# A fused attention and channel-mix kernel: a new hand-held order with more idle matmuls at the start, and last stores spread over two queues

## The chip, the core and the metric

The kernel runs on one core of a Trainium2 chip. The metric is the device time of one execution in microseconds; the time of a kernel is the median of its runs. The profile is one execution taken by the hardware profiler, and its times are counted from the start of that execution's span.

## What is computed

A linear attention with a normalised output feeds a channel mix with a squared ReLU and a sigmoid gate. The reference, cut to what matters:

```python
batch, n_heads, seq, head_dim = 8, 8, 576, 64      # d_model 512, d_ff 1024
kv  = einsum('bhsd,bhse->bhde', k, v)
att = einsum('bhsd,bhde->bhse', q, kv)
att = att / sqrt(mean(att * att, -1) + 1e-6) * g_norm
x   = att.transpose(0, 2, 1, 3).reshape(B, S, H * D)
x_prev = x shifted by one row of the sequence, zero at its start
xk = mu_k * x + (1 - mu_k) * x_prev
xr = mu_r * x + (1 - mu_r) * x_prev
kk  = maximum(xk @ w_k, 0)
out = sigmoid(xr @ w_r) * ((kk * kk) @ w_v)
```

All inputs and the output are float32 in memory; the loads issued by GpSimd (POOL) cast to bf16 on the way, and the matmuls run in bf16.

## The kernel before, in words

**Work and stages.** Attention runs batch by batch (b = 0 to 7), heads in four pairs (hp = 0 to 3). The channel mix runs over nine groups g of 512 rows, each group as soon as the batches that it needs are done. All bf16 tiles are held transposed, features on partitions.

- Loads: `load_q0.4` loads q of batch 0 from head 4 on (L281, POOL's queue). Batch 0 is loaded two heads at a time, batch 1 four heads at a time, later batches whole. Heads 0 and 1 of k and v of batch 0 come as float32 through SP's and ACT's queues (`early_k`, `early_v`, L291) and are cast on the chip (`cast_k`, `cast_v`, L294, by copy on L185 for ACT or L187 for VectorE, here DVE). `load_w_r`, `load_w_k`, `load_w_v` load each weight in two halves (L265).
- Attention of a head pair: `kv` is k transposed times v on TensorE (PE; L369 for batches 0 and 1, L354 later), `kvm` or `kvc` evicts it (L373, L361); `qT` transposes q on PE (L407, L412) and `qTc` evicts it (L416), from batch 3 on a DMA transpose on SP's queue does this (`qTd`, L395); `u` is q times kv (L431, L437), `uc` evicts it, in batch 0 scaled by g_norm (L456), `sq` squares it (L197, L199).
- Normalisation: in batch 0 `ss` sums the squares of a head pair with a matmul of ones (L482), `rs` is ACT's reciprocal root (L487), `x` multiplies (L491). Later batches do all four head pairs in one `st` (L520) and `rs` (L525), spread by the matmuls `sp` (L559) and multiplied by `x` (L564).
- Shift and blend: `d` is x minus the shifted x (L584, L585), `tk` and `tr` multiply it by mu (L191 on ACT, L193 on DVE), `xk` and `xr` add x (L595).
- Channel mix: `K` is xk times w_k (L630; K0.3 is group 0, feature block 3; blocks 0 to 3 need the first half of w_k, the others the second), `relu` (L634, ACT) and `sqk` (L637, DVE) follow; `R` is xr times w_r (L652), `sig` its sigmoid (L657, ACT); `V` is the square times w_v (L686, `a` with the first half of w_v, `b` with the second), `o` the product with the gate (L690, DVE), `S` the store (L616). In group 0 the R matmuls go head pair by head pair, so R0.0 needs only xr of head pair 0.

**What sets the order.** `ORDER`, a string of names, is the order in which the pieces are recorded, and each engine and queue runs its own in that order. After a name stand the engine (`A` ACT, `D` DVE, `S` SP) and the buffer slots: `qTc0.2:A:0` is on ACT and takes slot 0 of its tile. PSUM has four slots (`ps`), kv, q, k and v have two each, the float32 output tiles four. `Plan.run` (L96) only asks that what a piece needs stands before it and that the earlier users of a slot do. The costs in `add` (such as `{"ACT": 0.535, "DVE": 0.37}`) are a planner's; in this file only the order of the engines in such a dictionary has an effect, as the default where the name gives none.

**Idle matmuls.** `idle:28:0` issues 28 matmuls of a zero tile, 224 columns wide, into slot 0 of `ps`:

```python
def idle(n, slot):
    for _ in range(n):
        nc.tensor.matmul(tiles[("ps", slot)][:, 0, HS:512], zeros[:, 0:128], zeros[:, HS:512], start=True, stop=True)
```

Their result is never read. They wait for the zero tile (`zero`, L232) and for readers of the slot that they overwrite. Before the change there are 61 of them, in seven places, all ahead of R0.0.

**Stores.** A piece `S` stores 128 rows; in the last two groups it is cut in two (`.a`, `.b`), and each part can go to SP's or ACT's queue. In the last group each block of 128 rows has its own product, and the last block has two halves by columns (`o8.1.3.0`, `o8.1.3.1`).

Of the kernel before, what the change touches and what calls it, by code (L numbers as in the profile page):

```python
# [12 lines left out]


ORDER = """
    zero load_q1.4::0 ident load_v0.4::0 load_k0.4::0 early_k::0 g_load mu_r_load:A load_q0.4::1 idle:28:0 qT0.2::0 kv0.2::1
    ones kvm0.2::0 qT1.3::2 load_v0.6 load_k0.2 load_k0.6 load_q0.0 load_q0.6 load_v0.2 load_q0.2 load_v1.4::1 load_k1.4::1
    early_v::1 cast_v:A mu_k_load:S cast_k:A qTc0.2:A:0 kv0.0::3 u0.2::1 ident9 kvm0.0 mu_mm::0 mu sq0.2::0 qTc1.3:A:1 idle:9:3
    qT0.0::3 uc0.2:A:0 qTc0.0:D sel_load ss0.2::0 qT0.3::2 rs0.2::0 u0.0::1 qTc0.3:A idle:7:3 qT0.1::3 kv0.1::0 x0.2::0 d0.2::0
    tk0.2:D:0 qTc0.1:D sq0.0 ss0.0::2 rs0.0::1 kv0.3::3 kvm0.1 u0.1::0 qT1.2::2 sq0.1 uc0.0:D uc0.1:A load_q1.0 load_v1.0  # L20
    load_k1.0 idle:7:1 kv1.2::1 kvm0.3 x0.0 d0.0 tr0.0:D:1 u0.3::3 kvm1.2::1 tr0.2:D xk0.2 sq0.3 idle:3:0 u1.3::0 uc1.3:A:1
    ss0.1::1 rs0.1::0 uc0.3:D sel xr0.2 x0.1 d0.1 xr0.0 load_w_r0 qT1.0::0 ss0.3::3 qT1.1::1 qTc1.2:A qTc1.0:A rs0.3::1 qTc1.1:A
    tr0.1:D x0.3 idle:5:2 kv1.0::2 kvm1.0 d0.3 u1.2::0 tr0.3:A uc1.2:A xr0.1 load_w_r1 load_w_k0 idle:2:1 R0.0::31 u1.0::2 R0.1
    tk0.0:A tk0.3:D xk0.3 uc1.0:D xr0.3 xk0.0 tk0.1:D xk0.1 load_w_k1 R0.2 R0.3.1 R0.3.0 u1.1::0 sig0.0::0 sig0.1::1 uc1.1:D
    sq1.0:D:0 sq1.1:D K0.0::2 K0.1 K0.3::0 K0.2 st1::3 relu0.0::0 load_q2.0::1 load_w_v0 K0.5::1 sqk0.0::0 rs1::0 sp1.1::23
    x1.1.0::1 x1.1.1 load_w_v1 K0.4 K0.7::2 relu0.1::1 sqk0.1 relu0.2::0 sp1.0::03 K0.6 x1.0.0 x1.0.1 sqk0.2 qT2.2::1 relu0.3::1
    sqk0.3 V0.1a::0 V0.2a::3 qT2.1::2 V0.2b d1.0::0 qTc2.1:A:0 V0.3a qT2.3::2 tr1.0:A:1 d1.2 tr1.2:D xr1.2 xr1.0 V0.3b tk1.0:D:0
    o0.1::2 qTc2.3:A qT2.0::2 qTc2.0:A V0.0a load_k2.0::0 load_v2.0::0 R1.0::2 R1.1 kv2.0::3 tk1.2:A sig1.0::2 kvc2.0.0:A:0
    load_k3.0::1 load_v3.0::1 xk1.2 qTc2.2:D xk1.0 V0.0b kvc2.0.1:A K1.3::1 K1.2 V0.1b load_q3.0::0 qTd3::1 K1.6::2 o0.0::3
    relu1.1::0 kvc2.0.2:A u2.0::1 uc2.0:D:0 u2.1::3 uc2.1:A sq2.0:D:0 K1.7 u2.3::0 u2.2::3 relu1.3::1 uc2.2:A K1.4::1 K1.0::2  # L30
    K1.1 uc2.3:D sq2.1:D sqk1.3::1 sqk1.1 st2::0 rs2::1 relu1.0::1 sqk1.0 K1.5 relu1.2::0 R1.3::3 sp2.1::02 R1.2 load_q4.0::1
    V1.3a::1 V1.2a x2.1.1::0 x2.1.0 sqk1.2 sp2.0::20 sig1.1::1 x2.0.1 d2.2::0 tk2.2:A:1 load_v5.0::0 x2.0.0 V1.1a::3 V1.0a V1.0b
    kv3.0::0 load_v4.0::1 V1.3b V1.1b V1.2b d2.0 tk2.0:D xk2.0 xk2.2 K2.0::2 o1.0::1 kvc3.0.2:D:1 tr2.0:D:0 K2.1 K2.4::3 K2.5
    tr2.2:D xr2.2 relu2.0::1 xr2.0 kvc3.0.1:D sqk2.0::0 kvc3.0.0:D relu2.2::0 load_k4.0::0 K2.2::2 K2.3 R2.0::3 o1.1::0
    relu2.1::1 u3.0::0 u3.1::1 u3.2::2 R2.1 uc3.1:A:1 uc3.0:D sq3.0:A:0 sig2.0::0 R2.3::0 R2.2 sig2.1::2 u3.3::1 S1.2 qTd4::0
    uc3.2:D sqk2.2 sqk2.1 K2.6::2 kv4.0::3 load_v6.0::1 uc3.3:D sq3.1:D st3::1 S1.3 rs3::0 K2.7 kvc4.0.1:D:0 kvc4.0.2:D
    kvc4.0.0:D sp3.1::01 relu2.3::0 x3.1.1::1 x3.1.0 load_k5.0::1 V2.0a::3 V2.1a sp3.0::12 sqk2.3 u4.0::0 uc4.0:A:0 V2.1b x3.0.1
    S0.3 S0.2 x3.0.0 d3.2::0 d3.0 tk3.2:D:1 tr3.2:D:0 u4.3::2 u4.1::0 u4.2::1 uc4.1:A sq4.0:A:0 uc4.3:A uc4.2:A sq4.1:A V2.0b
    tr3.0:D xr3.2 load_q5.0::0 xr3.0 xk3.2 tk3.0:A V2.3a::0 V2.3b V2.2a V2.2b xk3.0 st4::2 rs4::1 R3.0::1 R3.1 K3.2::2 K3.3
    o2.1::0 o2.0::2 sig3.0::1 sp4.0::01 x4.0.1::0 x4.0.0 relu3.1::1 R3.2::3 R3.3 sp4.1::12 x4.1.1 K3.1::0 K3.0 x4.1.0 K3.5::2  # L40
    K3.7::1 K3.4 K3.6 d4.2::0 tk4.2:A:0 relu3.0::0 sig3.1::2 d4.0 tk4.0:D xk4.2 sqk3.1::1 xk4.0 kv5.0::0 relu3.2::1 sqk3.0
    relu3.3::0 kvc5.0.0:D:1 K4.2::3 K4.4::2 K4.5 K4.3 K4.7::1 K4.6 kvc5.0.1:A tr4.2:D:1 tr4.0:A sqk3.2 xr4.0 sqk3.3 qTd5::1 S2.2
    S2.3 S1.0 load_k7.0::0 load_k6.0::1 relu4.1::1 relu4.3::0 kvc5.0.2:D xr4.2 sqk4.1::0 relu4.2::1 sqk4.2 K4.1::3 K4.0
    relu4.0::1 V3.3a::0 V3.2a load_v7.0::0 load_q6.0::1 load_q7.0::0 u5.3::1 u5.1::2 V3.2b uc5.3:D:1 uc5.1:A u5.0::3 u5.2::1
    uc5.2:D sqk4.0 uc5.0:A sq5.0:D:0 V3.3b R4.3::2 o3.1::0 sqk4.3 S1.1 S0.1 S3.2 R4.2 sq5.1:A st5::3 rs5::0 V3.0a::1 sp5.0::03
    sig4.1::0 V3.0b V3.1a x5.0.1::1 x5.0.0 sp5.1::30 kv6.0::2 V3.1b x5.1.0 x5.1.1 d5.2::0 tk5.2:A:0 d5.0 tk5.0:D xk5.2 V4.3a::3
    R4.1::0 R4.0 V4.3b V4.2a kvc6.0.0:A:0 sig4.0::2 xk5.0 K5.2::0 V4.2b tr5.0:A:1 kvc6.0.1:A K5.3 tr5.2:A relu5.1::1 S0.0
    qTd6::0 o3.0::1 o4.1::3 S3.3 kvc6.0.2:D K5.0::1 xr5.2 K5.1 K5.6::3 relu5.0::0 sqk5.0::1 u6.1::2 u6.0::0 uc6.1:A:0 uc6.0:A
    K5.7 V4.1a::1 V4.1b u6.2::2 u6.3::0 relu5.3::0 uc6.2:A xr5.0 sq6.0:D:0 sqk5.1 uc6.3:D sq6.1:D V4.0a V4.0b o4.0::0 st6::3
    kv7.0::2 rs6::1 sp6.1::03 x6.1.0::0 x6.1.1 sqk5.3 kvc7.0.2:D:1 kvc7.0.1:D R5.1::1 R5.0 K5.5::0 K5.4 sig5.0::1 kvc7.0.0:D  # L50
    relu5.2::1 sp6.0::31 R5.2::2 R5.3 sig5.1::0 sqk5.2 x6.0.0 x6.0.1 d6.0::0 tk6.0:D:0 xk6.0 tr6.0:A:1 d6.2 tk6.2:D V5.1a::0
    xk6.2 V5.2a::3 V5.2b V5.1b qTd7::1 u7.2::2 u7.3::1 uc7.3:A:1 S4.1 S4.2 S3.1 S2.0 S2.1 S4.0 S4.3 uc7.2:A sq7.1:A:0 V5.0a
    V5.0b u7.1::1 u7.0::2 uc7.1:A uc7.0:A sq7.0:D V5.3a tr6.2:D o5.0::2 xr6.2 xr6.0 K6.3::1 K6.1::2 V5.3b o5.1::0 K6.2
    relu6.1::0 K6.0 relu6.0::1 sqk6.1::0 sqk6.0 K6.5::0 K6.4 st7::1 rs7::0 K6.6::3 K6.7 R6.2::2 relu6.2::0 S3.0 relu6.3::1
    sqk6.2 sp7.0::10 R6.3 x7.0.0::1 sqk6.3 x7.0.1 sig6.1::2 V6.2a::3 R6.0::1 sp7.1::02 x7.1.1 d7.2::0 x7.1.0 V6.3a V6.3b
    V6.1a::2 V6.2b V6.0a R6.1 V6.0b V6.1b d7.0 tk7.2:D:0 tk7.0:D xk7.2 tr7.0:D:1 xk7.0 sig6.0::1 o6.1::3 K7.3::0 K7.2 tr7.2:A
    relu7.1::0 sqk7.1::1 K7.4::1 K7.5 relu7.2::1 sqk7.2 o6.0::1 S6.2 S6.3 K8.0::3 K8.3::0 K8.2 S5.1 S5.0 S6.0 S6.1 K7.0::1
    relu8.1::0 sqk8.1::0 xr7.0 xr7.2 K8.1 K7.1 relu8.0::1 relu7.0::0 K8.4::2 sqk7.0 K7.7::0 K7.6 R8.2::3 R8.3 sig8.1::0
    relu7.3::0 sqk7.3 sqk8.0 R7.2::1 R7.3 sig7.1::2 R7.1::3 R7.0 K8.5 relu8.2::0 V7.2a::0 S5.3 V7.3a V7.3b K8.6::1 R8.0::2 K8.7
    V7.2b sig7.0::1 S5.2 relu8.3::1 o7.1::3 S7.3.b:S S7.2.a:A sqk8.2 V8.0a::3 V7.1a::1 sqk8.3 R8.1 V7.1b sig8.0::2 V7.0a  # L60
    V8.1a::0 V8.1b o8.0.1.0::2 V7.0b S8.1.1.0.a:S o7.0::1 V8.0b o8.0.0.0 V8.2a::2 V8.2b V8.3.0a::0 V8.3.0b V8.3.1a::1 V8.3.1b
    S7.0.a:A S8.0.0.0.b:A S7.0.b:A S7.1.b:A S8.1.1.0.b:S S7.2.b:S S7.1.a:S S8.0.0.0.a:S S7.3.a:S o8.1.2.0::0 S8.2.2.0.a:A
    S8.2.2.0.b:A o8.1.3.0 S8.3.3.0.a:A S8.3.3.0.b:S o8.1.3.1 S8.3.3.1.a:S S8.3.3.1.b:A
"""


# [51 lines left out]
def kernel(  # L118
# [499 lines left out]
    def mix(g):  # L618
# [73 lines left out]
        for c2 in range(2):  # L692
# [18 lines left out]
            for xs, cs, ms, tag, ps in todo:  # L711
                w = (xs[1] - xs[0]) * (cs.stop - cs.start)
                dv = add(f"o{g}.{c2}{tag}", {"DVE": 0.07 + 1.06 * w / 1024},
                         lambda _, xs=slice(*xs), ps=ps, sg=sg, ot=ot, cs=cs: v_mul(_, xs, ps, sg, ot, cs), deps=ms + [sg_done], bufs=[ps, sg, ot])
                for x in range(*xs):
                    ci = 2 * c2 + x
                    rows = runs(g, ci)
                    for i, part in enumerate([rows] if g < NG - 2 else [[r] for r in rows]):
                        on = {"SP": 0.53 * len(part)}
                        if g >= NG - 2:  # L720
                            on["ACT"] = 0.45
                        add(f"S{g}.{ci}{tag}" + (f".{'ab'[i]}" if g >= NG - 2 else ""), on,
                            lambda eng, ci=ci, ot=ot, x=x, cs=cs, part=part: store(eng, g, ci, get(ot)[:, x, :], cs, part), deps=[dv],
                            bufs=[ot], land=0.64 * sum(n for _, n in part) / 128 * (cs.stop - cs.start) / C)
# [44 lines left out]
```

## Time and profile before

| | us |
|---|---|
| median of 7 runs (210.82 to 212.48) | 211.81 |
| the profiled execution | 212.13 |
| its span | 210.3 |
| PE busy | 196.6 |
| DVE busy | 140.4 |
| ACT busy | 124.1 |
| first matmul of the channel mix's R (L652) | 27.21 |
| first matmul of its K (L630) | 31.38 |
| end of the last matmul | 204.19 |

The page cuts the span into 40 slices of 5.26 us; a digit is the busy share of an engine in a slice in tenths. PEclk is the TensorE clock that was granted, in tenths of the full one. Groups of rows are named by line, engine and tiles; `ps L630` is what line 630 writes. The timeline has start, duration, engine, line and tiles of instructions, neighbours of one kind merged; a `q` after the engine is its queue, which issues transfers, and the bracket is the idle time before and what ended it. A windows row has the stretch, its length, then busy time and count of each engine, the clock, the DMA share and the GB/s. A transfer's landing is given as us after its issue.

### The profile page before, as it was taken

The numbers are of one execution on the slowest core, as the hardware profiler recorded it, in microseconds if no ns is written. First come the engines' busy times: TensorE is split into PE (matmuls) and PEld (weight loads), VectorE is DVE, ScalarE is ACT, GpSimd is POOL, SyncE is SP. The second block draws the span as 40 slices with busy tenths as digits, with TensorE's granted clock in tenths as the row PEclk, the third lists the DMA queues.
The fourth block names the chain that finished last, engine by engine and source line by source line (L and its number), as shares of the span: only waits on it lengthen the run. The fifth ranks groups of instructions, "written<-read, shape, count | busy, mean of one in ns | idle before, by whom it ended". The sixth has DMA issues, their size and how long they took to land.

```text
span 210.3 us, 3834 instructions
## 1 busy us (share of the span) xinstructions
PE 196.6 (93%) x1538; PEld 98.2 (47%) x1559; DVE 140.4 (67%) x259; ACT 124.1 (59%) x149; POOL 29.4 (14%) x46
## 2 busy tenths in 40 slices
PE   7299999999999999999999999999999999999980
PEld 6276654445335444434783444354443444444440
DVE  2017995994959988988957794878685957122360
ACT  2245879487792386892977778765678065361100
POOL 7893530011002005000410000000000000000000
PEclk9857999999999999999999999999999999999996
DMA  6999999999980979998799998048100035400274
GB/s 147 190 197 203 205 205 206 206 201 203 191 100 5 174 154 181 195 205 102 146 195 260 219 229 122 0 126 225 51 0 0 3 111 169 123 3 0 62 209 127
DMA packets 39317, 29.71 MB, mean 141 GB/s; under 512 B 13564, under 2 KB 34820, under 8 KB 39300
## 3 DMA queue, kind: packets, MB, share of 16 engines
q0 software_dynamic: 21248, 16.48, 51.7%
q1 hardware_dynamic: 17020, 11.45, 24.3%
q10 hardware_dynamic: 1032, 1.54, 2.6%
q8 instruction: 12, 0.20, 0.4%
q14 instruction: 5, 0.04, 0.1%
HBM read 33.56 MB, written 9.44 MB: 204 GB/s over the span
## 4 chain that ended last, share of the span: by engine, by line
PE 89%; DMA 3%; ACT 2%; issue 2%; POOL 1%; DVE 1%; POOLq 0%
PE ps L630 30%; PE ps L686 29%; PE ps L652 14%; DMA q<-in_q_dram 3%; PE ps L354 3%; PE ps L437 2%; PE ps L736 2%; PE ps L407 2%; PE ps L369 2%; PE ps L559 2%; PE ps L431 1%; PE ps L520 1%; ACT sq L197 1%; PE ps L482 1%; ACT L205 1%
## 5 line engine op out<-in xcount | busy, mean ns | idle before, releaser
L686 PE MATMUL ps<-w_v,sqk 128*128 128x512 bf16 (+1 forms) x285 | 65.8, 373 | 0.9 <-issue 0.6
L630 PE MATMUL ps<-xk,w_k 128*128 128x512 bf16 (+1 forms) x313 | 65.7, 358 | 0.7 <-issue 0.5
L634 ACT ACTIVATE relu<-ps 128x1024 bf16<-128x1024 f32 x36 | 36.4, 1022 | 25.5 <-PE ps L630 17.2
L630 PEld LDWEIGHTS <-w_k 128*128 128x128 bf16 x320 | 30.3, 98 | 30.4 <-issue 1.6
L686 PEld LDWEIGHTS <-sqk 128*128 128x128 bf16 x296 | 27.5, 98 | 31.0 <-issue 1.4
L637 DVE TENSOR_TENSOR sqk<-relu 128x1024 bf16<-128x1024 bf16 x36 | 24.3, 687 | 16.5 <-ACT relu L634 16.5
L652 PE MATMUL ps<-w_r,xr 128*128 128x512 bf16 x141 | 34.2, 380 | 0.3 <-issue 0.2
L690 DVE TENSOR_TENSOR out<-ps,sig 128x1024 f32<-128x1024 f32 (+2 forms) x21 | 22.3, 1068 | 17.0 <-issue 10.8
L657 ACT ACTIVATE sig<-ps 128x1024 bf16<-128x1024 f32 x18 | 18.3, 1021 | 13.9 <-PE ps L652 13.7
L564 DVE TENSOR_TENSOR xT<-uT,ps 128x576 bf16<-128x576 bf16 x28 | 20.1, 750 | 6.6 <-PE ps L559 5.9
L191 ACT ACTIVATE t<-d,mu_sb 128x576 bf16<-128x576 bf16 x24 | 17.4, 767 | 10.3 <-DVE d L585 10.3
L652 PEld LDWEIGHTS <-xr 128*128 128x128 bf16 x144 | 13.3, 98 | 16.4 <-DVE xr L595 0.7
L185 ACT CAST uT<-ps 128x576 bf16<-128x576 f32 x18 | 11.0, 635 | 5.1 <-PE ps L437 5.0
L193 DVE TENSOR_SCALAR t<-d,mu_sb 128x576 bf16<-128x576 bf16 x40 | 13.2, 373 | 0.3
L595 DVE TENSOR_TENSOR xr<-t,xT 128x1152 bf16<-128x1152 bf16 (+1 forms) x18 | 11.9, 685 | 1.4 <-ACT t L191 1.4
L585 DVE TENSOR_TENSOR d<-xT 128x1152 bf16<-128x1152 bf16 (+1 forms) x18 | 12.4, 691 | 0.6
L281 POOL DMA_DIRECT2D v<-in_v_dram x11 | 7.9, 715 | 33.4 <-PE ps L354 32.3
L595 DVE TENSOR_TENSOR xk<-t,xT 128x1152 bf16<-128x1152 bf16 (+1 forms) x18 | 12.2, 687 | 0.3
L736 PE MATMUL ps<-zeros 128*128 128x224 bf16 x61 | 10.4, 339 | 1.2 <-DVE zeros L232 1.2
L281 POOL DMA_DIRECT2D q<-in_q_dram x12 | 8.6, 720 | 19.6 <-PE ps L412 13.5
L281 POOL DMA_DIRECT2D k<-in_k_dram x11 | 7.9, 716 | 22.0 <-PE ps L354 18.8
L187 DVE CAST uT<-ps 128x576 bf16<-128x576 f32 x10 | 7.5, 756 | 3.4 <-PE ps L437 3.1
(60 smaller groups left out, 137.3 us busy)
## 6 DMA issues: line engine op xcount, KB each, us to landing
out_dram<-out SPq DMA_DIRECT2D x20, 192.0 KB
q<-in_q_dram POOLq DMA_DIRECT2D x6, 576.0 KB, 14.9
k<-in_k_dram POOLq DMA_DIRECT2D x6, 576.0 KB, 14.8
v<-in_v_dram POOLq DMA_DIRECT2D x6, 576.0 KB, 11.3
out_dram<-out SPq DMA_DIRECT2D x20, 128.0 KB
out_dram<-out SPq DMA_DIRECT2D x23, 64.0 KB
w_k<-in_moe_w_k_dram POOLq DMA_DIRECT2D x2, 512.0 KB, 13.6
w_v<-in_moe_w_v_dram POOLq DMA_DIRECT2D x2, 512.0 KB, 16.3
```

Source lines behind the costliest of these rows:

```text
L191: nc.scalar.mul(out=dst, in_=src, mul=by)
L281: nc.gpsimd.dma_start(out=get(kvq[(n, b)])[:, h0:h1, :], in_=rows(n, b, h0, h1))
L564: nc.vector.tensor_tensor(out=get(xT)[:, 2 * i:2 * i + 2, NP + c:NP + c + HS], in0=flat(slice(2 * i, 2 * i + 2))[:, :, c:c + HS], in1=get( ...
L595: nc.vector.tensor_tensor(out=dst[:, hsl, c0:c0 + S], in0=get(t[key])[:, hsl, :], in1=get(xT)[:, hsl, 0:S], op=ALU.add)
L630: nc.tensor.matmul(get(ps)[:, fc % 2, a0:a1], w_k_sb[:, cc, 128 * fc:128 * fc + 128], xk[:, cc, x0:x0 + a1 - a0], start=(cc == 0), stop=(c ...
L634: nc.scalar.activation(out=get(rt), in_=get(ps), func=AF.Relu)
L637: nc.vector.tensor_mul(out=get(sqk)[:, 2 * f2:2 * f2 + 2, :], in0=get(rt), in1=get(rt))
L652: nc.tensor.matmul(get(ps)[:, ci % 2, :], xr[:, cc, c:c + 128], w_r_sb[:, cc, :], start=(cc == 0), stop=(cc == NHP - 1))
L657: nc.scalar.activation(out=get(sg), in_=get(ps), func=AF.Sigmoid)
L686: nc.tensor.matmul(get(ps)[:, ci % 2, cs], get(sqk)[:, fc, 128 * ci:128 * ci + 128], w_v_sb[:, fc, cs], start=(fc == 0), stop=(fc == NFC - 1))
L690: nc.vector.tensor_mul(out=get(ot)[:, xs, cs], in0=get(ps)[:, xs, cs], in1=get(sg)[:, xs, cs])
L736: nc.tensor.matmul(tiles[("ps", slot)][:, 0, HS:512], zeros[:, 0:128], zeros[:, HS:512], start=True, stop=True)
```

## The change

Only `ORDER` and two of the planner's costs change. The pieces are the same ones, each once, apart from the idle matmuls: 79 in ten places instead of 61 in seven, again all but one ahead of R0.0 (the one stands before R0.2).

- The first real work on PE is kv0.0, from the early loads, and then head pair 0; it was q's transpose and kv of head pair 2. `idle:28:0` stays first, and `idle:12:1` follows kv0.0.
- POOL's queue starts with k, q and q of heads 2, 2 and 0 of batch 0, and batch 1's first q comes seventh; it was first. `load_w_r0` stands before the k and v loads of batch 1; it stood behind them.
- The small loads swap queues: `mu_r_load` goes to SP, ahead of `early_k`, and `mu_k_load` to ACT, behind `early_v`, which is now ACT's first transfer. `cast_k` and `cast_v` go from ACT to DVE.
- ss, rs, x, d, t and the blends of batch 0 run in the order of head pairs 0, 1, 2, 3; they ran 2, 0, 1, 3. kv1.2, kv1.0, qT1.0, u1.2 and u1.3 now stand behind R0.0.
- Later stages keep their pieces in a new order of loads, stores, slots and engines. At the end the halves of a store go to SP and ACT in turn, and group 7's first product comes earlier than group 8's first.

The core of the diff (the start and the end of `ORDER`, and the costs):

```diff
-    zero load_q1.4::0 ident load_v0.4::0 load_k0.4::0 early_k::0 g_load mu_r_load:A load_q0.4::1 idle:28:0 qT0.2::0 kv0.2::1
-    ones kvm0.2::0 qT1.3::2 load_v0.6 load_k0.2 load_k0.6 load_q0.0 load_q0.6 load_v0.2 load_q0.2 load_v1.4::1 load_k1.4::1
-    early_v::1 cast_v:A mu_k_load:S cast_k:A qTc0.2:A:0 kv0.0::3 u0.2::1 ident9 kvm0.0 mu_mm::0 mu sq0.2::0 qTc1.3:A:1 idle:9:3
-    qT0.0::3 uc0.2:A:0 qTc0.0:D sel_load ss0.2::0 qT0.3::2 rs0.2::0 u0.0::1 qTc0.3:A idle:7:3 qT0.1::3 kv0.1::0 x0.2::0 d0.2::0
...
+    zero load_k0.2::0 early_v::0 mu_r_load:S early_k::1 mu_k_load:A g_load load_q0.2::0 load_q0.0 load_v0.2::0 load_v0.6
+    load_q0.4::1 load_q1.4::1 ident ones cast_k:D cast_v:D idle:28:0 kv0.0::0 sel_load kvm0.0::0 load_v0.4 load_k0.4 load_k0.6
+    load_q0.6 idle:12:1 qT0.0::1 qTc0.0:D:0 idle:7:0 u0.0::2 ident9 mu_mm::3 mu qT0.1::0 uc0.0:D:0 qTc0.1:D load_q1.0 kv0.1::1
+    qT0.2::3 qTc0.2:A kvm0.1 sq0.0::0 idle:9:0 ss0.0::0 rs0.0::0 u0.1::1 sq0.1 qT1.3::3 kv0.2::2 load_w_r0 kvm0.2 uc0.1:D
+    idle:3:0 kv0.3::0 load_k1.4::1 load_v1.4::1 qTc1.3:A:1 ss0.1::2 qT0.3::3 u0.2::1 rs0.1::1 sq0.2 x0.0::0 d0.0::0 sel kvm0.3
+    qTc0.3:A uc0.2:D load_w_r1 x0.1 tr0.0:D:0 d0.1 idle:5:2 ss0.2::2 rs0.2::0 x0.2 xr0.0 idle:2:0 u0.3::0 sq0.3 idle:10:1
+    ss0.3::3 uc0.3:A rs0.3::1 x0.3 d0.2 tr0.2:D qT1.2::1 qT1.1::2 tr0.1:D xr0.1 load_k1.0 load_v1.0 load_w_k0 load_w_k1
+    tk0.0:A:1 qTc1.2:A qTc1.1:A idle:2:0 R0.0::03 qT1.0::1 kv1.2::2 load_q2.0::0 R0.1 qTc1.0:D d0.3 xr0.2 idle:1:1 R0.2 tk0.1:A
...
-    V7.2b sig7.0::1 S5.2 relu8.3::1 o7.1::3 S7.3.b:S S7.2.a:A sqk8.2 V8.0a::3 V7.1a::1 sqk8.3 R8.1 V7.1b sig8.0::2 V7.0a
-    V8.1a::0 V8.1b o8.0.1.0::2 V7.0b S8.1.1.0.a:S o7.0::1 V8.0b o8.0.0.0 V8.2a::2 V8.2b V8.3.0a::0 V8.3.0b V8.3.1a::1 V8.3.1b
-    S7.0.a:A S8.0.0.0.b:A S7.0.b:A S7.1.b:A S8.1.1.0.b:S S7.2.b:S S7.1.a:S S8.0.0.0.a:S S7.3.a:S o8.1.2.0::0 S8.2.2.0.a:A
-    S8.2.2.0.b:A o8.1.3.0 S8.3.3.0.a:A S8.3.3.0.b:S o8.1.3.1 S8.3.3.1.a:S S8.3.3.1.b:A
...
+    V8.1a::1 sig8.0::1 sig7.0::2 V7.0b V7.1a V7.1b o7.0::2 S7.0.b:A V8.0a::3 R7.2::0 V7.2a::2 S6.3 S7.1.b:S S6.2 S5.3 S6.1
+    S7.0.a:S R7.3 V8.0b o8.0.0.0::3 sig7.1::2 S7.1.a:S V7.3a V7.3b V7.2b o7.1::1 S8.0.0.0.a:A V8.2a::0 V8.2b V8.1b V8.3.0a::3
+    V8.3.0b V8.3.1a::2 V8.3.1b S7.2.b:A S7.2.a:S S8.0.0.0.b:S o8.1.2.0::0 S8.2.2.0.a:A S7.3.b:S S8.2.2.0.b:A o8.0.1.0
+    S8.1.1.0.a:S S7.3.a:S S8.1.1.0.b:A o8.1.3.0 S8.3.3.0.b:A S8.3.3.0.a:S o8.1.3.1 S8.3.3.1.a:S S8.3.3.1.b:A
...
-                        on = {"SP": 0.53 * len(part)}
+                        on = {"SP": 0.5 * len(part)}
                         if g >= NG - 2:
-                            on["ACT"] = 0.45
+                            on["ACT"] = 0.55
```

## The prediction

> **What bounds the kernel now.** I read the 40 slices first, then the head by windows, its waits and rows, then the tail. TensorE is full from slice 3 on, so three things set the end: when the dense matmuls begin, their sum, and what follows the last one.
>
> ```profile
> PE   7299999999999999999999999999999999999980
> ...
> PEclk9857999999999999999999999999999999999996
> ```
>
> The granted clock dips in slices 2 to 4. TensorE's longest wait (total us, times, longest) comes before it:
>
> ```profile
> PE ps L407 <- DMA q<-in_q_dram: 3.8, 1, 3.8
> ```
>
> The windows (stretch; PE, PEld, DVE, ACT, POOL busy, then clock, DMA share, GB/s) tell why:
>
> ```profile
> 5.10:8.50 3.40, 0.82 (x9) 0.56 (x6) 0.00 (x0) 1.48 (x2) 2.77 (x6) 1.00 1.27 185
> 8.50:11.90 3.40, 2.20 (x48) 2.20 (x48) 0.36 (x2) 0.64 (x1) 2.87 (x5) 0.50 1.30 197
> 11.90:15.30 3.40, 3.40 (x27) 2.11 (x25) 0.46 (x2) 1.82 (x3) 3.10 (x6) 0.50 1.28 195
> 15.30:18.70 3.40, 3.40 (x33) 2.01 (x29) 1.93 (x5) 1.86 (x3) 1.33 (x2) 0.50 1.31 203
> 18.70:22.00 3.30, 3.30 (x70) 2.37 (x71) 2.68 (x8) 1.93 (x3) 1.70 (x3) 1.00 1.30 203
> ```
>
> The first 28 idle matmuls end at 5.9, TensorE then waits 3.8 us for a q load, and from 8.5 to 18.7 it has half the clock. That delays the chain from q to xk, which ends here (PE, then DVE):
>
> ```profile
> 31.38 1.24 PE L630 MATMUL ps<-xk,w_k 128*128 128x512 bf16 x5
> ```
>
> ```profile
> 30.89 0.46 DVE L595 TENSOR_TENSOR xk<-t,xT 128x576 bf16<-128x576 bf16 x1
> ```
>
> K0.0, the first channel-mix matmul, starts at 31.38, just as the last blend ends (30.89 + 0.46 = 31.35). DVE was busy 4.60 and 4.86 us of the two 5 us windows before 30. Its other input came earlier:
>
> ```profile
> L265 POOL DMA_DIRECT2D w_k<-in_moe_w_k_dram x2: 740/744/747, 15.1 to 16.6; - x2
> ...
> DMA to landing us min/median/max: 13.0/13.6/14.3
> ```
>
> So w_k halves land at 15.1 + 13.0 = 28.1 and 16.6 + 14.3 = 30.9; by the same view w_v lands at 36.1 and 38.9. From 31.38 to 204.19 TensorE is busy 170.72 of 172.81 us. The tail:
>
> ```profile
> 204.22 0.42 DVE L690 TENSOR_TENSOR out<-ps,sig 128x256 f32<-128x256 f32 x1 [0.45 <-PE ps L686]
> 204.29 0.83 ACTq L616 DMA_DIRECT2D out_dram<-out  x1
> ...
> 206.38 0.32 ACTq L616 DMA_DIRECT2D out_dram<-out  x1
> ...
> 206.79 0.42 ACTq L616 DMA_DIRECT2D out_dram<-out  x1
> ```
>
> The last output is ready at 204.64, but ACT's queue, free at 205.12, issues its last two stores only at 206.38 and 206.79. The span ends at 210.3.
>
> **What the Trainium skill says.** "TensorE: Matmul & The Clock Gate", What's actually happening: the array idles at half clock, one busy window of 3.4 us releases it, one idle window takes it back. The trace agrees: full to about 8.5 although TensorE stopped at 5.9, then half for three such windows; a 24%-busy window (0.82 of 3.40) counted as idle. The same page, Part 4, says that transposes do not count as busy; that fits the window 8.5 to 11.9, mostly transposes and small matmuls, which did not release it. "DMA: Bandwidth & Descriptors", Issuing engines are not separate DMA queues: stores from SP and ACT share the same engines, two queues save issue time only. The tail moved 273 GB/s between 204 and 206, so I credit no bandwidth.
>
> **The change part by part.**
>
> *First work and the gap.* kv0.0 now comes first; its k and v need the two early loads and two DVE casts. The early v landed at about 5.0 (ACT's cast began then); swapping the two queues' small loads moves either by at most 0.6. A DVE cast of this shape is in no row: between 0.4 (plain bf16 moves of this size) and 0.83 (ACT's). "VectorE: DVE Perf Modes", The perf-mode tier table, gives 1227 ns for 2048 fp32 elements, an estimate of 0.46 for 768; I take it. kv0.0 starts at 5.0 + 2 x 0.46, near 6.0. Twelve idle matmuls at 0.096 (start to start, the last of the first 28; the first ones, at half clock, 0.187) carry TensorE to 7.7. The next need, q0.0, is now third in POOL's queue. Single two-head loads landed 0.74 apart; the first, double-sized one landed at 7.25. So k0.2, q0.2 and q0.0 land near 6.5, 7.25 and 8.0. The largest break shrinks from 3.8 to 0.4 us, and the window 5.1 to 8.5 is about 75% busy. I take it that the clock stays full.
>
> *TensorE from qT0.0 to R0.0.* Warm durations from rows after 18.7: transposes 0.35 x 7, kv 0.40 x 3, u and ss 0.26 x 8, mu 0.3, 38 idle matmuls at 0.096 3.65: 9.7 us. The idle ones wait for the tile that they overwrite, and ss waits for ACT (square 0.65 and rs 0.65, one pair per head pair): 1.6 us more by following ACT's queue, in which a copy of 0.64 stands ahead of most squares. R0.0 starts near 19.3; it was 27.21. Five pieces of batch 1 (kv1.2, kv1.0, qT1.0, u1.2, u1.3, about 2.5 us) that stood ahead of R0.0 now stand behind it, so K0 gains less.
>
> *DVE.* rs0.3 ends near 19.5. After it DVE has eighteen steps to the last xk at their spacing in the trace: x 0.37, two d 1.16, four t 1.16, three xr 1.11, four xk 1.48, qTc1.0 0.38, two kvm 0.66, uc1.3 0.67: 7.0 us, 26.5. One kvm waits for kv1.0, hence for v1.0, which now lands last before w_k, at 28.1 - 2.6 = 25.5; that puts the last xk at 27.4.
>
> *Transfers.* POOL's order changes, but the bytes ahead of w_k (batch 0, batch 1, w_r) are the same, and the DMA share never left 1.27 to 1.31 from 5 us on. So w_k still lands at 28.1. It is now the last to come: K0 starts at 28.1 instead of 31.38, a gain of 3.3. If loads land 0.3 sooner and DVE at 27.4 binds, 3.9; if ACT's chain slips a us, 2.3. The 18 more idle matmuls (79 against 61) cost 1.7 us of TensorE under the waits for ACT and loads; without this cover they cost 1.7.
>
> *After K0.* The matmuls are the same set, and all idle ones stand ahead, so 172.8 us again. The next landings: w_k's second half 30.9, needed at K0 + 4.1 = 32.2; w_v 36.1, needed at K0 + 8.4 = 36.5; its second half 38.9, needed 40.3; k2.0, now the second of its pair as v2.0 was (issued 24.60, landed 20.1 later), at 44.7, needed by kv2.0 at 44.5. So only 0.2 is lost, and gaining more than 3.7 at the head would just move the wait there. Reordering inside the 172.8 could give at most its 2.1 us of idle, or lose as much; I take 0, range -1.0 to +1.5.
>
> *Tail.* Each store uses one of eight completion semaphores in turn and waits for the store that used it before. The program's order shows ACT's 206.38 store tied to one issued at 202.34. In the new order group 7's first half is stored well before, and ACT's last store is tied to one issued 1.9 us before the last matmul's end T. By the semaphore events stores there took about 3.6 us to land, so it goes at T + 1.7, not T + 2.6: a gain of 0.9. Bounds: nothing if bandwidth sets it, 1.7 if it goes when its data is ready. The planner's two store costs (0.53 to 0.5, 0.45 to 0.55) change no instruction. The new SP order (SP's transposes among stores) has slack: qTd3 waits for q3.0, landing at 53.4, and u3 runs at 28.1 + 39 = 67.
>
> *Sum.* The profiled execution took 212.13 (span 210.3 and 1.83 around it), 0.32 above the median of 211.81. 212.13 - 3.3 - 0.9 = 207.9; against the median, 207.6.
>
> **Rivals.**
> 1. *The gain is given back in the middle.* POOL is in order: load_v7.0 waits for kv5.0 (about 98) and holds k6.0 two places behind, which kv6.0 needs near 115. In the before trace such loads landed 7.2, then 4 to 5 us apart; that makes 115, just in time, and one more store burst costs 1 to 2.5. For: no slack. Against: few stores are queued there now. 209.3.
> 2. *The clock drops once more at 8.5 and returns at 18.7.* For: nothing shows a 75% window. TensorE does 5.6 of the 8.7 us up to ss0.3 by 18.7, ends it at 22.4, rs0.3 at 23.1, xk at 30.6: K0 gains 0.7: 211.81 - 0.7 - 0.9 = 210.2.
> 3. *Slower: idle matmuls at half clock become the bound.* Same drop, but not released before about 25.5. Every idle matmul then costs 0.187, TensorE reaches ss0.3 at 25.2, rs0.3 26.3, xk 33.9, K0 34: 2.6 later than before, 211.81 + 2.6 - 0.9 = 213.5. It decides once the half clock lasts beyond 22 to 23. Against: 15.3 to 18.7, no fuller, released it.
> 4. *It does not do what it says:* the breaks stay, since loads and ACT set them, and nothing moves: 211.8.
>
> **How the numbers follow.** Main case 0.66, 207.6, own range 206.3 to 208.7 (head 2.3 to 3.9, tail 0 to 1.7, middle within 1.0, not all at once). Rival 1 0.14, rival 2 0.07, rival 3 0.07, rival 4 0.03, a better middle below 206.3 0.03. Range 206.3 to 209.8 leaves out rivals 2 to 4 and the last, 0.20. Half a per cent (1.06 us, about what a measurement of this kernel can tell from no change) makes faster 0.90, same 0.03, slower 0.07.
>
> **What would show it.** Right: clock 1.00 from about 5 to the end of the matmuls; the largest PE wait before R0.0 under 1 us; first L630 matmul at 28.1 within half a us of w_k's landing; 172.8 us from there to the last L686; last ACT store under 2 us after it. Wrong: clock 0.50 after 8.5, w_k not the last to come at K0, a PE wait over 1 us on k6 or k2 loads, or stores still landing 4.5 us after T.

## The result and the profile after

| us | before | after |
|---|---|---|
| median (runs) | 211.56 (31) | 208.28 (12) |
| lowest to highest | 210.25 to 212.93 | 207.66 to 209.25 |
| the profiled execution | 212.13 | 207.92 |
| its span | 210.27 | 206.12 |
| first matmul of R, R0.0 | 27.21 | 19.71 |
| first matmul of K | 31.38 | 27.80 |
| end of the last matmul | 204.19 | 200.80 |
| from the first K matmul to there | 172.81 | 173.00 |
| from the last matmul to the span's end | 6.08 | 5.31 |

The ratio of the medians is 0.985, its 95% interval 0.982 to 0.987: faster by 3.3 us, where 4.2 was forecast. The two profiled executions differ by 4.21; the section on the prediction accounts for the difference. Ratios below are to runs of before made alongside (medians 211.46 to 211.49); one run each of new_tail and new_tail2 was in a slower state and is left out.

The 40 slices of after, TensorE's busy tenths and its clock:

```profile
PE   7989989999999999999999999999999999999990
...
PEclk9999999999999999999999999999999999999998
```

The dip of the clock in slices 2 to 4 is gone, and TensorE is at 8 or 9 tenths from the second slice to the last but one. The windows of the head (the columns are those of the windows shown for before):

```profile
6.35:9.76 3.41, 3.41 (x49) 2.71 (x47) 1.10 (x4) 0.00 (x0) 3.33 (x7) 1.00 1.29 194
9.76:13.17 3.41, 2.90 (x62) 2.55 (x64) 1.55 (x4) 1.57 (x3) 3.20 (x6) 1.00 1.33 204
13.17:16.58 3.41, 3.02 (x58) 2.07 (x53) 2.37 (x7) 2.54 (x6) 2.08 (x4) 1.00 1.27 199
```

The clock stays at 1.00 with TensorE 85 to 100% busy. Its waits (total us, times, longest):

```profile
PE ps L736 <- DVE qT L187: 0.5, 1, 0.5
...
PE ps L407 <- DMA q<-in_q_dram: 0.3, 1, 0.3
PE ps L482 <- ACT sq L197: 0.3, 1, 0.3
PE ps L630 <- ACT sig L657: 0.2, 1, 0.2
```

The wait of 3.8 us for q is 0.3, and no other wait inside the work is over 0.5. The timeline where the channel mix begins:

```profile
26.73 1.94 ACT L657 ACTIVATE sig<-ps 128x1024 bf16<-128x1024 f32 x2
26.78 0.82 DVE L595 TENSOR_TENSOR xk<-t,xT 128x576 bf16<-128x576 bf16 x2
...
27.80 0.81 PE L630 MATMUL ps<-xk,w_k 128*128 128x512 bf16 x3 [0.22 <-ACT sig L657]
```

The last xk ends at 26.78 + 0.82 = 27.60. The first of the two sigmoids ends at 27.75 and frees a PSUM slot, which the bracket names as K's last wait. The loads of w_k:

```profile
L265 POOL DMA_DIRECT2D w_k<-in_moe_w_k_dram x2: 745/747/749, 15.4 to 16.5; - x2
...
DMA to landing us min/median/max: 11.7/12.5/13.2
```

The first half lands at 15.4 + 11.7 = 27.1 by these rounded figures (27.16 by the events of the trace). So three chains end within 0.6 us of each other: w_k at 27.16, xk at 27.60, the sigmoid at 27.75. Each hides the others, and whichever is late sets K.

### The profile page after: what moved, and what is told of

It reads as the page before. It is cut to its first block, busy times and chain, and to the rows that moved or that the text cites. A ratio compares the mean times of both kernels' runs of the same rounds, so it can differ in the third digit from the quotient of the medians.

```text
span 206.1 us, 3872 instructions
## 1 busy us (share of the span) xinstructions
PE 195.9 (95%) x1554; PEld 98.2 (48%) x1577; DVE 141.0 (68%) x258; ACT 121.1 (59%) x148; POOL 29.9 (15%) x46
## 4 chain that ended last, share of the span: by engine, by line
PE 85%; POOL 3%; DMA 3%; DVE 3%; issue 2%; ACT 2%; ACTq 0%; DVEq 0%; POOLq 0%
PE ps L686 31%; PE ps L630 30%; PE ps L652 14%; DMA q<-in_q_dram 3%; PE ps L354 3%; PE ps L437 2%; PE ps L559 2%; POOL q L281 1%; PE ps L520 1%; POOL k L281 1%; POOL v L281 1%; PE ps L736 1%; ACT uT L185 1%; PE ps L412 0%; ACT sig L657 0%
## 5 line engine op out<-in xcount | busy, mean ns | idle before, releaser
L630 PE MATMUL ps<-xk,w_k 128*128 128x512 bf16 (+1 forms) x312 | 66.4, 358 | 0.9 <-issue 0.3
L191 ACT ACTIVATE t<-d,mu_sb 128x576 bf16<-128x576 bf16 x29 | 20.7, 768 | 13.6 <-DVE d L585 13.6
L185 ACT CAST uT<-ps 128x576 bf16<-128x576 f32 x19 | 11.7, 641 | 10.0 <-PE ps L437 9.1
L736 PE MATMUL ps<-zeros 128*128 128x224 bf16 x79 | 11.7, 306 | 1.7 <-DVE zeros L232 1.2
L187 DVE CAST uT<-ps 128x576 bf16<-128x576 f32 x9 | 6.8, 757 | 7.8 <-PE ps L437 7.8
L193 DVE TENSOR_SCALAR t<-d,mu_sb 128x576 bf16<-128x576 bf16 x35 | 11.6, 374 | 0.1
L736 PEld LDWEIGHTS <-zeros 128*128 128x128 bf16 x79 | 8.6, 115 | 3.3 <-DVE zeros L232 1.2
```

Source lines behind the costliest of these rows:

```text
L191: nc.scalar.mul(out=dst, in_=src, mul=by)
L630: nc.tensor.matmul(get(ps)[:, fc % 2, a0:a1], w_k_sb[:, cc, 128 * fc:128 * fc + 128], xk[:, cc, x0:x0 + a1 - a0], start=(cc == 0), stop=(c ...
```

## The experiments

Theory: the gain comes from TensorE's clock, which stays full since nothing as idle as before's 24% window is left, and the new order of POOL's and DVE's work only lets the earlier matmuls reach K. Rivals: the new order itself makes K early, and the idle matmuls do nothing; or a good part of the gain is made by the last stores.

**Which part of the change carries the gain.** `bridge` keeps the old order and adds idle matmuls where TensorE waited 3.8 us:

```
- idle:28:0 qT0.2::0
+ idle:28:0 idle:38:0 qT0.2::0
```

> The old order with 38 more idle matmuls behind the first 28, so that TensorE works through the 3.8 us in which it waited for q; nothing else is changed. If the half clock between 8.5 and 18.7 is what delayed K0: clock 1.00 from 5 us on, the transposes of q at 9.7 as before, the first x near 14.3 instead of 17.0, K0.0 at 28.4 to 29.0: 2.4 to 3.0 us faster, ratio 0.986 to 0.989. Rival, that the order of loads and of the head pairs is what counts: K0.0 after 30.5, under 1 us faster, ratio over 0.995.

Measured: 208.81, ratio 0.988 (0.985 to 0.990). The clock is full from 3.89 on, K starts at 28.30, the last xk ends at 28.27, w_k landed at 27.40. The window that holds what is left of the wait stays at full clock:

```profile
7.30:10.71 3.41, 2.66 (x58) 2.41 (x57) 0.15 (x1) 1.01 (x2) 2.58 (x4) 1.00 1.28 189
```

One insertion into the old order gives 2.6 of the 3.3 us. `no_idle` is the counterpart, the new order with no idle matmul:

```
- cast_v:D idle:28:0 kv0.0::0
+ cast_v:D kv0.0::0
... (and the nine others taken out)
```

> The new order with no idle matmuls at all. If they are what makes the new order fast: TensorE starts at half clock near 6.1 with its first kv and gets the full clock only when real work fills a window, after 20; K0.3 at 31 to 33, ratio 0.997 to 1.008. Rival, that loads, ACT and DVE set the head whatever the clock: K0.3 below 29.5, ratio under 0.992.

Measured: 211.81, ratio 1.001 (1.000 to 1.003); K starts at 31.24. TensorE now has no work before the first k and v:

```profile
PE ps L370 <- DVE v L188: 6.4, 1, 6.4
```

The records give no clock ahead of 25.75, and a window without a record is printed as 1.00. The transposes tell it, by one window each of no_idle, before and after (transposes alone; PE, PEld, clock):

```profile
8.69:12.10 3.41, 1.39 (x24) 1.11 (x24) 1.00 1.30 195
...
8.48:11.89 3.41, 1.38 (x24) 1.11 (x24) 0.50 1.30 197
...
9.76:13.17 3.41, 1.11 (x35) 0.89 (x36) 1.00 1.33 204
```

24 of them took as long as at half clock in before, where 35 took 1.11 us at full clock in after; one transpose took 281 ns up to the last at 24.33, against 206 ns at full clock. So it had half the clock up to 25.75. Without any idle matmul the new order is no faster than the old one with its 61; one insertion into the old order gives 2.6 us, the whole change 3.3. The filled clock carries most of the gain, as the theory says. The last 0.7 is the new order's, as far as is known: the intervals of bridge and of the full change overlap, and the two profiles (208.66 and 207.92) split their 0.74 into K 0.50 earlier, 0.19 lost behind it and about 0.4 at the end. The old order with no idle matmul at all was not run.

**How much must be filled.** `only28` is the new order with just the first 28:

```
- idle:12:1 ... idle:7:0 ... idle:9:0 ... idle:3:0 ... idle:5:2 ... idle:2:0 ... idle:10:1 ... idle:2:0 ... idle:1:1
```

> The new order with the first 28 idle matmuls alone; the 51 others are left out. If the bridging ones are needed to hold the clock: clock 0.50 from about 9.8 for two or more windows of 3.4 us, K0.3 at 29 to 31, 1.5 to 3 us slower than the whole change, ratio to before 0.991 to 1.0. Rival, that real work in the new order is dense enough by itself: clock 1.00 throughout and K0.3 at 27.8, the same time as the whole change, ratio 0.985.

Measured: 210.47, ratio 0.996 (0.993 to 0.998); K at 30.07. With the clock at half for 13.65 us, against 10.24 in before, the new order is still 0.9 us faster, so it is worth something without a full clock too. Its windows:

```profile
4.49:7.90 3.41, 1.80 (x30) 1.47 (x30) 1.34 (x3) 0.00 (x0) 3.33 (x8) 1.00 1.22 175
7.90:11.31 3.41, 2.13 (x52) 1.69 (x51) 2.07 (x6) 0.69 (x2) 3.23 (x5) 1.00 1.29 194
11.31:14.72 3.41, 2.85 (x40) 2.13 (x39) 0.36 (x2) 2.25 (x4) 2.75 (x4) 0.50 1.32 204
```

The clock outlives the first window, 53% busy, and is lost after the second, which is busier. The same two windows for the transposes of line 408 alone (stretch; PE, PEld, clock):

```profile
4.49:7.90 3.41, 0.13 (x6) 0.13 (x8) 1.00 1.22 175
7.90:11.31 3.41, 1.21 (x36) 0.81 (x34) 1.00 1.29 194
```

Without transposes the windows hold 1.67 us (49%, kept) and 0.92 us (27%, lost). That agrees with the sentence of the Trainium skill that the prediction drew on ("TensorE: Matmul & The Clock Gate", Part 4), that transposes don't count as busy. It rests on this one pair of windows; the transposes alone were not varied. `one_break` opens only the place of the twelve:

```
- load_q0.6 idle:12:1 qT0.0::1
+ load_q0.6 qT0.0::1
```

> The new order without the 12 idle matmuls between kv0.0 and the transposes of q; TensorE then stands still there for 1.3 us, and the window of 3.4 us around it is 60 to 65 % busy. If one short break is enough to lose the clock: 0.50 for at least two windows and 1 to 2 us slower than the whole change, ratio 0.989 to 0.994. Rival, that only a nearly idle window loses it (0.82 of 3.4 us did, in the profile of before): clock 1.00, the time of the whole change, ratio 0.984 to 0.986; the 12 matmuls then do nothing.

Measured: 207.95, ratio 0.983 (0.980 to 0.985), not to be told from the full change. One window and two waits:

```profile
6.30:9.70 3.40, 2.54 (x44) 1.92 (x43) 0.96 (x5) 0.00 (x0) 3.33 (x7) 1.00 1.30 196
```

```profile
PE ps L409 <- DMA q<-in_q_dram: 0.9, 1, 0.9
...
PE ps L632 <- DMA w_k<-in_moe_w_k_dram: 0.2, 1, 0.2
```

A 75% window (58% without transposes) with a break of 0.9 us keeps the clock, so these twelve matmuls do nothing for it; K starts 0.28 sooner (27.52), and now waits for w_k, landed at 27.48. `bridge16` puts 16 instead of 38 into the old order:

```
- idle:28:0 qT0.2::0
+ idle:28:0 idle:16:0 qT0.2::0
```

> The old order with 16 idle matmuls behind the first 28 instead of the 38 that fill the wait for q; 1.5 to 3 of the 3.8 us of standing still remain, depending on when the clock comes up. If part of a window of work holds the clock, as the new order without its 12 showed: clock 1.00 from the start in most runs and the time of the full bridge, ratio 0.987 to 0.990. Rival, that the break must be filled: clock 0.967 to 0.985 over the span as in before, ratio 0.995 to 1.0.

Measured: 208.88, ratio 0.989 (0.986 to 0.992), K at 27.96. TensorE still waits 1.7 us for q, its window is 60% busy (2.05 us, no transposes), and the clock stays:

```profile
5.72:9.13 3.41, 2.05 (x21) 1.79 (x19) 0.00 (x0) 1.56 (x2) 2.74 (x6) 1.00 1.24 175
```

So the break need not be closed, only its window filled by about half. `late_fill` looks for the limit from below, the new order without the twelve and the next seven and nine:

```
- load_q0.6 idle:12:1 qT0.0::1   ...   idle:7:0   ...   idle:9:0
+ load_q0.6 qT0.0::1   ...
```

> The new order without the 12, 7 and 9 idle matmuls that come second, third and fourth; the 23 later ones stay. With all 51 gone the clock fell after a window with 2.1 of 3.4 us of transposes and small matmuls. If that stretch is where filling counts: the clock falls near 9.5 to 12, K0.3 at 28.5 to 30, ratio 0.988 to 0.995. Rival, that the later ones counted: clock 1.00, K0.3 at 27.5, ratio 0.982 to 0.985.

Measured: 209.72 (208.31 to 211.09, 15 runs), ratio 0.991 (0.989 to 0.994): on the edge. Its profiled execution is its best (208.31):

```profile
4.68:8.09 3.41, 2.02 (x35) 1.64 (x34) 1.48 (x4) 0.00 (x0) 3.34 (x7) 1.00 1.27 186
8.09:11.51 3.42, 1.69 (x40) 1.39 (x40) 2.06 (x6) 1.19 (x2) 3.17 (x6) 1.00 1.30 197
11.51:14.92 3.41, 3.36 (x39) 2.16 (x40) 0.87 (x2) 1.75 (x3) 3.18 (x5) 0.50 1.31 201
```

The transposes take 0.45 and 0.87 us of the first two, which leaves 46% (kept) and 24% (lost, for one window). The mean clock of its 15 runs goes from 0.991 (208.3 us) over 0.980 (209.3) to 0.969 (211.0). A window at half clock takes 0.008 off the mean of such a run (half of 3.41 in 207 us), so each that is lost costs about 1 us here. Where the windows begin differs from run to run (the last section has the figures), which is the likely reason for the spread; it was not controlled. new_tail, below, has the old head, and its profile closes in on the limit from the other side, with a window of 41% and no transposes that lost the clock:

```profile
4.00:7.41 3.41, 1.40 (x14) 1.14 (x12) 0.00 (x0) 1.57 (x2) 3.02 (x5) 1.00 1.17 154
7.41:10.82 3.41, 0.83 (x20) 0.83 (x22) 0.00 (x0) 0.09 (x1) 2.47 (x4) 0.50 1.29 188
```

**The joint of the halves.** `new_head` records the new order up to the first K and the old one from there (against the new one):

```
  xk0.0 R0.3.0 u1.1::2 u1.0::1
- K0.3::3 K0.2 sig0.0::1 uc1.1:D sq1.1:D:0 uc1.0:A ...
+ uc1.0:D sig0.0::1 uc1.1:D sq1.0:D:0 sq1.1:D K0.0::2 ...
```

> The new order up to the piece before K0.3, then the old order for all that is left. If the head carries the gain, as the prediction says: K0.3 at 27.5 to 28.2 (31.38 before, 27.80 with the whole change), then 172.8 us to the last matmul, and the old tail of 6.1 us: about 3.4 us faster than before, ratio 0.984. Rival, that the reordering of the middle and the tail carries it: under 1.5 us faster, ratio over 0.993, although K0.3 starts early, because the old order then waits for loads or buffers.

Measured: 209.41, ratio 0.990 (0.988 to 0.993). K starts only at 29.41, because the joint makes it wait for a slot:

```profile
PE ps L632 <- DVE uT L189: 1.5, 1, 1.5
```

`new_head2` has the joint three pieces of K later:

```
  sq1.0:D st1::0 rs1::0 K0.0::2
- sp1.0::10 K0.1 relu0.1::0 K0.6::3 ...
+ K0.1 relu0.0::0 K0.5::1 sqk0.0::0 ...
```

> The new order up to the piece before K0.0 (with K0.3, K0.2 and st1 inside it), then the old order. The first try at this joint made its first K wait 1.5 us for a slot. If the head carries the gain and that wait was of the joint's making: K0 starts near 27.8, 172.8 to 173.3 us to the last matmul, the old tail of 5.7 to 6.1: 207.6 to 208.7, 3.0 us faster than before, ratio 0.984 to 0.987. Rival, that the old order cannot use an earlier start: K0 early, but over 174 us after it, ratio over 0.990 as in the first try.

Measured: 209.24, ratio 0.991 (0.987 to 0.994). K starts at 27.80 as with the full change, but V, 8.43 us behind it in before, now comes 9.33 behind, and from the first K to the last matmul it takes 174.02. That is not the old order failing to use an early start:

| us | K starts | V behind K | first K to last matmul |
|---|---|---|---|
| before (old order) | 31.38 | 8.43 | 172.81 |
| bridge (old order) | 28.30 | 8.43 | 172.81 |
| bridge16 (old order) | 27.96 | 8.42 | 173.10 |
| new_head | 29.41 | 8.42 | 172.80 |
| new_head2 | 27.80 | 9.33 | 174.02 |
| after (new order) | 27.80 | 8.73 | 173.00 |

With K only 0.16 us later, bridge16 loses 0.3 behind it, not 1.2. So the loss is of the mixed order at the joint, where TensorE waits for a square (0.4, as in after) and then for ACT's relu (0.2), among others; neither half run measures the head alone.

**The tail.** `new_tail` has the old order up to K8.0 and the new one after (against the old one):

```
  sqk7.2 o6.0::1 S6.2 S6.3
- K8.0::3 K8.3::0 K8.2 S5.1 S5.0 S6.0 ...
+ S5.0 S5.1 S5.2 K8.0::2 K8.1 relu8.0::0 ...
```

> The old order up to the piece before K8.0, then the new order. If the tail is worth what the prediction gave it: 0.9 us faster, ratio 0.996, with the last store landing 3.9 us after the last matmul (4.5 before). Rival, that the tail is set by how fast the stores are moved: under 0.3 us, ratio over 0.998. With the head's 3.4 us the parts should add up to the whole.

`new_tail2` puts first all stores of groups 5 and 6 that are still owed at the joint:

```
- S5.0 S5.1 S5.2 K8.0::2 K8.1 ...
+ S5.1 S5.0 S6.0 S6.1 S5.3 S5.2 K8.0::2 K8.1 ...
```

> The old order up to the piece before K8.0, then the stores of groups 5 and 6 that are still owed, then the new order. The first try at this left those stores behind group 7's, and DVE and TensorE waited 3 us for output tiles. If storing group 7 early is what the new tail gains: the last store lands 3.9 us after the last matmul, the span ends 5.3 to 5.5 us after it, no wait over 1 us from K8.0 on; 0.4 to 0.9 us faster, ratio 0.996 to 0.998. Rival, that the tail as a whole is worth nothing: ratio 0.9985 to 1.002.

Measured: ratio 1.021 (1.016 to 1.026; 214.53 to 217.62), and ratio 1.019 (1.014 to 1.024; 213.94 to 217.06). Both are slower. The second has this wait for an output tile, which the first has too, and which neither parent order has:

```profile
PE ps L631 <- DVE out L691: 3.0, 1, 3.0
```

Both take 176.46 us from K to the last matmul, 3.65 more than before, and 5.50 us after it. So neither shows by its time what the new stores are worth. `alt_queues` lets the last 15 stores of the old order alternate between ACT and SP, nothing else:

```
- S8.0.0.0.b:A S7.0.b:A S7.1.b:A S8.1.1.0.b:S
+ S8.0.0.0.b:S S7.0.b:A S7.1.b:S S8.1.1.0.b:A
... (the others likewise)
```

> The old order with the last fifteen stores given to ACT and SP in turn, nothing else. If issuing on two queues in turn is what the new tail gains: last store issued under 1.5 us after the last matmul, 0.4 to 0.9 us faster, ratio 0.996 to 0.998. Rival, that the bytes still to be stored at the end set it, and the new tail gains by having stored group 7 earlier: within 0.3 us, ratio 0.9985 to 1.0015.

Measured: 211.94, ratio 1.002 (1.000 to 1.004). Sharing the queues evenly gains nothing (in its profile 6.23 us follow the last matmul). That leaves a comparison across profiles, five with the old last stores and five with the new:

| last matmul to the span's end, us | | mean |
|---|---|---|
| old stores: before, bridge, bridge16, new_head, new_head2 | 6.08, 5.69, 5.83, 5.82, 5.51 | 5.79 |
| new stores: after, one_break, only28, late_fill, no_idle | 5.31, 5.41, 5.60, 5.39, 5.46 | 5.43 |

So about 0.35 us is the new tail's part, not the 0.77 of the one pair; the 5.50 of new_tail and new_tail2 lie with the new ones. It is a comparison of whole kernels: no run here isolates the stores.

## Why the prediction was right, and where it was off

*First work and the gap.* Right in what mattered: the largest break fell from 3.8 to 0.5, and the clock stayed full. The sizes were off. The two casts:

```profile
5.31 0.56 DVE L187 CAST k<-out 96x768 bf16<-96x768 f32 x1 [2.69 <-DMA out<-in_k_dram]
5.78 0.68 DVE L187 CAST v<-out 96x768 bf16<-96x768 f32 x1
...
6.51 0.53 PE L369 MATMUL ps<-v,k 96*64 96x128 bf16 x12
```

The casts started at 5.3 rather than 5.0 and took 0.56 and 0.68 rather than 0.46 (inside the bounds of 0.4 and 0.83; the estimate scaled the whole time of a longer cast by size), so kv0.0 began at 6.5, not 6.0. q0.0 landed at 7.28, not 8.0, and the twelve idle matmuls then held TensorE until 8.23: here they cost a little instead of hiding anything, as one_break showed.

*TensorE to R0.0.* 19.71 against 19.3. In one_break, without the twelve that held TensorE until 8.23, it was 19.25, so the late start is enough to account for the difference.

*DVE and transfers.* The step "w_k still lands at 28.1. It is now the last to come" failed. In before it landed at 28.12, but the other five profiles with the old head spread from 27.40 (bridge) to 28.45 (new_tail), so 28.1 was one execution's; the seven with the new head have it between 27.16 and 27.48. The forecast's other branch came true ("If loads land 0.3 sooner and DVE at 27.4 binds, 3.9"): the last xk ended at 27.60, and ACT's sigmoid, which the prediction did not list, at 27.75. The head gained 3.58 where 3.3 was forecast, between the bounds of 2.3 and 3.9.

*After K0.* 173.00 against 172.81: 0 was right within 0.2. "The same set" is not a sufficient reason, though: new_head2, with the same matmuls in a mixed order, lost 1.2 us there.

*Tail.* Right in kind, too large in size. The timeline of after:

```profile
200.84 0.42 DVE L690 TENSOR_TENSOR out<-ps,sig 128x256 f32<-128x256 f32 x1 [0.45 <-PE ps L686]
...
201.94 0.33 ACTq L616 DMA_DIRECT2D out_dram<-out  x1
```

ACT's last store goes 1.1 us after the last matmul, where 1.7 was forecast. By the events of the trace the store that it shares a semaphore with was complete at 201.86, so it went 0.08 later; in before the pair is 206.30 and 206.38. The tie is real, but the change did not move it: the earlier store of the pair was issued 1.85 us before the last matmul's end in before (202.34) and in after (198.95), and 1.84 in bridge (199.27). What differs is how long that store took to land, 4.0 us in before and 2.9 in after; in bridge, with the old ties, it took 3.0, and the tied store went at 1.25 after the last matmul too. The new order's own part is that no ACT store follows the tied one, where before and bridge have one more, 0.41 and 0.42 us later. "A gain of 0.9" was read from one slow landing; about 0.35 is the order's.

*Sum.* The profiled pair gives 3.58 - 0.19 + 0.82 = 4.21 (the tail here up to the device time), the forecast 4.2. That they meet is luck: the head gained 0.28 more than forecast, the rest 0.27 less. The medians give 3.3. The mis-sized term is the start that both were read from: 212.13 was taken as 0.32 above the median, 0.57 by 31 runs. The mean clock of 81 runs of before lies near three values, 0.981 (29 runs, 210.9 us on average), 0.975 (26, 211.5) and 0.968 (26, 212.0). The profiled execution, at 0.967 with three half-clock windows, is of the dearest kind, so that a typical run had less to win. The profile of after (207.92) in turn lies 0.36 below its median; all its runs have a clock of 0.993 to 1.000, so this is not the clock. 0.57 + 0.36 is the 0.93 between 4.21 and the medians' 3.28.

*Rivals.* The gain given back at kv6.0: no wait there. The clock lost at 8.5, or idle matmuls as the bound: no, in all 12 runs; one_break shows that even the 75% window would have kept it. That it does nothing: no.

## What to carry to other kernels

Where a profile shows a dip of the clock, look for the window ahead of it that is emptier than half, not counting transposes, and put in just enough idle matmuls for that one: 16 at the right place in the old order brought 2.6 us of the 3.3. Once such a stall is gone, the gain is capped by the next chains, here three within 0.6 us, so list all of them, ACT's too, before pricing it. And a stall that depends on where such a window falls has a different size from run to run: price it from several executions, not from the profiled one.

## What the runs showed of the hardware

- Windows that held 46, 49, 51, 52 and 60% of matmuls other than transposes (PE's busy time less that of the transposes) kept the clock (late_fill, only28, one_break, after, bridge16); windows with 16, 24, 25, 27 and 41% lost it (alt_queues, late_fill, before, only28, new_tail). In these traces the limit lies between 41 and 46%.
- The clock stayed at half for 3.41, 6.83, 10.24 and 13.65 us, that is one to four windows (late_fill, new_tail2, before, only28). It first became full between 3.89 us (bridge) and 6.84 us (new_tail2), though the first idle matmul started at 1.19 or 1.20 in every profile that has one: the windows do not begin at a fixed point of the kernel.
- What gives the clock back stays open. In before a window with 3.42 us busy (0.32 of it transposes) from 11.89 to 15.31 was followed by another at half clock, in late_fill one with 3.36 us (0.69) was followed by full clock at once. So "one busy window of 3.4 us releases it", which the prediction took over, did not hold in before.
- A VectorE cast from float32 to bf16, 96x768, took 0.56 and 0.68 us.
- A store that shares a completion semaphore with an earlier one was issued 0.08 us after that one was complete, in before, bridge and after alike; landing took 2.9 to 4.0 us for these.
